# A weight piece's rounding term on GpSimd, five first loads on ScalarE's queue, and the input flag at step 88

## The chip, the cores and the metric

The kernel runs on one core of a Trainium2 chip. A core has five engines that run their own instruction queues in order: TensorE (PE in the profile; PEld is its weight load), VectorE (DVE), ScalarE (ACT), GpSimd (POOL) and SyncE (SP), which here only issues DMA transfers. The metric is the device time of one execution in microseconds (us); lower is better. Before the change it is 751.67 us, the median of 3 runs (749.25 to 754.2).

## The reference

Attention with a local window and a few global columns is followed by a feed-forward part with a gelu. There are 4 batches of 768 positions, 8 heads of 64, d_model 512 and d_ff 2048; the weights w_in and w_out are float64.

```python
scores = scale * np.matmul(q, k.transpose(0, 1, 3, 2))
is_global = pos[None, :] < int(n_global)
is_local = (rel >= 0) & (rel < int(n_local))
bias = -slopes[:, None, None] * dist[None, :, :]
scores = np.where(is_global | is_local, scores + bias, -1e9)
a = np.exp(scores - np.max(scores, axis=-1, keepdims=True))
a = a / (np.sum(a, axis=-1, keepdims=True) + 1e-09)
x = np.matmul(a, v)                      # heads side by side: 3072 x 512
h = x @ w_in
g = 0.5 * h * (1.0 + erf(h * inv_sqrt2))
return (g @ w_out).astype(np.float32)
```

## The kernel before

**Chunks and steps.** The 3072 positions are cut into 12 chunks of 256 (c), and the hidden 2048 columns into 8 slices of 256 (s). A step is one chunk with one slice: 96 steps, numbered T. In each step PE makes h = x·w_in for the slice (`m1`, L461, 24 matmuls), ScalarE makes the gelu gr (L471), GpSimd the rounded part gh (`hi_pool`, L145), VectorE the rest gl = gr − gh (L151), and PE adds both into the chunk's two accumulators (`m2`, L491, 24 matmuls). m1 runs one step ahead of m2. After a chunk's last slice ScalarE copies an accumulator to a tile o (L497) and issues its output transfer (L498). The tiles with the tag "o" share two buffers.

**Splitting.** Every product is made of three matmuls of a rounded part (hi) and a rest (lo) of each operand. Chunks 0 and 1 (`NATIVE`) do the attention in plain float32 instead. Attention for a chunk is scores (L332 in the first two chunks), row maximum on VectorE (L341), exponentials on ScalarE (L356), transposes on PE (L382), the copy pt to SBUF on ScalarE (L385 in the first two chunks), the product with v (av, L410), and for the later chunks a scaling by GpSimd (L369).

**The opening.** Steps 0 to 3 take the slices 0 and 1 of chunks 0 and 1, and the next twelve alternate between these chunks, so that each weight slice is used by both. Meanwhile the weights arrive: 32 pieces (8 slices of 4 pieces, w0_0 to w7_3, 512 KB each) of 64-bit words, loaded by SP (L156) into four buffers for the slices 0 to 6. `split_weights` turns a piece into float32: L180 takes the low words, reads them as unsigned numbers and scales them to the rounding term; L182 and L184 cut and shift the bits of the high words into a tile wb on VectorE; L186 adds the rounding term, so it waits for L180; ScalarE copies the result into its hi form (L192); VectorE subtracts (L151). SP's next load of a piece waits until L186 and L184 have read the buffer's last content.

**The limits and the flag.** n_local and n_global are loaded to all partitions (L55) and made into a penalty for the scores. The fast path holds only for certain inputs, so VectorE collects the largest row maximum (nmax) and a check over the weights' words (wand; the words are loaded a second time, c<-w, and checked at the even steps up to 80). `flag` reduces both to one number: a chain on VectorE (wmin, mx, ok, bad), a transpose on PE (flag_ps, L596), and three more steps on VectorE to flag_i. All engines then load flag_i (L750) and branch on it (L751) past a general path that isn't taken here.

**What sets the order.** The tile framework's scheduler orders each engine's instructions by its own model of time; within that, waits between engines are semaphores. Its decisions change with the code, so instructions that the source doesn't touch may move too.

The DECODE table gives the step in which the pieces of a slice are split (−6, −4, … 8), and START the step at which each chunk's attention begins.

Of the kernel before, what the change touches and what calls it, by code (L numbers as in the profile page):

```python
# [10 lines left out]
I32 = mybir.dt.int32  # L11
U32 = mybir.dt.uint32
AF = mybir.ActivationFunctionType
ALU = mybir.AluOpType
PSUM = bass.MemoryType.PSUM

B, H, S, D = 4, 8, 768, 64
P = 128
# [5 lines left out]
CT = 256  # L24
# [24 lines left out]
def dap(t, off, dims):  # L49
    return bass.AP(tensor=t.tensor, offset=t.offset + off, ap=[list(d) for d in dims])  # L50


def load_scalars(nc, pool, src, name):
    w = pool.tile([P, 2, 2], I32, name=name + "_w")
    nc.sync.dma_start(w.rearrange("p i t -> p (i t)"), src.bitcast(I32).partition_broadcast(P))  # L55
    f = pool.tile([P, 2, 2], F32, name=name + "_f")
    nc.vector.tensor_copy(f, w)
    r = pool.tile([P, 2], F32, name=name)
    lo, hi = f[:, :, 0], f[:, :, 1]
    nc.vector.scalar_tensor_tensor(out=r, in0=lo, scalar=0.0, in1=hi, op0=ALU.is_lt, op1=ALU.add)  # L60
    nc.vector.scalar_tensor_tensor(out=r, in0=r, scalar=4294967296.0, in1=lo, op0=ALU.mult, op1=ALU.add)
    return r[:, 0:1], r[:, 1:2]
# [6 lines left out]
class Fast:  # L69
# [30 lines left out]
    def consts(self):  # L100
        nc, const = self.nc, self.const
        self.nl, self.ng = load_scalars(nc, const, self.limits, "nn")
        self.ident = const.tile([P, P], F32, name="ident")
        make_identity(nc, self.ident)
# [62 lines left out]
    def split_weights(self, s):  # L167
        nc = self.nc
        if s == LATE:
            self.early.close()  # L170
            self.wts = self.ctx.enter_context(self.tc.tile_pool(name="wlate", bufs=1, side="right"))
        if s == NST - 1:
            self.words.close()
            self.wts = self.ctx.enter_context(self.tc.tile_pool(name="wlast", bufs=1))
        for nm, dst, shape in (("win", self.win, [P, 4, 256]), ("wout", self.wout, [P, 2, 512])):
            dst[s] = tuple(self.wts.tile(shape, F32R, name=f"{nm}{k}{s}") for k in "hl")
        for i in range(4):
            w = self.raw.pop((s, i, "w"))
            lw, hw = w[:, :, 0], w[:, :, 1]
            nc.scalar.activation(out=lw, in_=lw.bitcast(U32), func=AF.Copy, scale=2.0 ** -29)  # L180
            a = self.sm.tile([P, 512], I32, name=f"wb{s}_{i}", tag="o")
            nc.vector.tensor_scalar(out=a, in0=hw, scalar1=0x07FFFFFF, scalar2=3,  # L182
                                    op0=ALU.bitwise_and, op1=ALU.logical_shift_left)
            nc.vector.scalar_tensor_tensor(out=a, in0=hw, scalar=-0x40000000, in1=a,  # L184
                                           op0=ALU.bitwise_and, op1=ALU.bitwise_or)
            nc.vector.tensor_tensor(out=a, in0=a, in1=lw, op=ALU.add)  # L186
            af = a.bitcast(F32)
            if i < 2:
                hi, lo = (x[:, 2 * i:2 * i + 2, :].rearrange("p d f -> p (d f)") for x in self.win[s])
            else:  # L190
                hi, lo = (x[:, i - 2, :] for x in self.wout[s])
            nc.scalar.copy(hi, af)  # L192
            self.lo_dve(lo, af, hi)
# [21 lines left out]
    def load_qk(self, c, p):  # L215
        nc = self.nc
        b, cc = divmod(c, CPB)
        k0 = (b * H + 2 * p) * D * S
        first = cc == 0
        nb = 1 if first else 2  # L220
        if c in NATIVE:
            kr = self.es.tile([P, nb, 256], F32, name=f"kr{c}_{p}", tag="kn", bufs=4)
            qr = self.es.tile([P, CT], F32, name=f"qr{c}_{p}", tag="qn", bufs=4)
            if first:
                nc.sync.dma_start(kr[:, 0, :], dap(self.kT, k0, [[S, P], [1, 256]]))
            else:
                nc.sync.dma_start(kr[:, :, NG:256], dap(self.kT, k0 + cc * CT - 96, [[S, P], [P, 2], [1, 224]]))
                nc.sync.dma_start(kr[:, :, 0:NG], dap(self.kT, k0, [[S, P], [0, 2], [1, NG]]))
            nc.sync.dma_start(qr, dap(self.qT, k0 + cc * CT, [[S, P], [1, CT]]))
            self.raw[c, p] = (kr, qr, nb)  # L230
            return
        if p == 0 and (cc == 1 or c == len(NATIVE)):
            self.load_glob(b)
        kr = self.stg.tile([P, 2, nb, 256], F32, name=f"kr{c}_{p}", tag="stage", padded_shape=[P, 2, 2, 256])
        qr = self.stg.tile([P, 2, CT], F32, name=f"qr{c}_{p}", tag="qraw", bufs=1)
        for u in (0, 1):
            ps = slice(u * 64, u * 64 + 64)
            if first:
                nc.sync.dma_start(kr[ps, :, 0, :], dap(self.kT, k0, [[S, D], [D * S, 2], [1, 256]]))
            else:  # L240
                for j in range(2):
                    nc.sync.dma_start(
                        kr[ps, :, j, NG:256],
                        dap(self.kT, k0 + cc * CT + j * P - 96, [[S, D], [D * S, 2], [1, 224]]))
            nc.sync.dma_start(qr[ps], dap(self.qT, k0 + cc * CT, [[S, D], [D * S, 2], [1, CT]]))
        self.raw[c, p] = (kr, qr, nb)
# [285 lines left out]
                    if r == rr:  # L532
                        self.exps(c, bt)

    def run(self):
        self.load_qk(0, 0)
        self.consts()
        last = NCH * NST
        for c in NATIVE:
            for p in range(NP):  # L540
                if (c, p) != (0, 0):
                    self.load_qk(c, p)
                self.load_v(c, p)
            if c == 0:
                for s in range(3):
                    self.load_weights(s)
        for s in range(3, NST - 1):
            self.load_weights(s)
        for self.T in range(START[0] - 1, last):
            T = self.T  # L550
            for s in range(NST):
                if T == DECODE[s]:
                    if s == NST - 1:
                        self.load_weights(s)
                    self.split_weights(s)
            if 16 <= T < 80 and T % 2 == 0:
                self.check_load((T - 16) // 2)
            if 18 <= T < 82 and T % 2 == 0:
                self.check_words((T - 18) // 2)
            if 0 <= T + 1 < last:  # L560
                self.m1(T + 1, 0)
            self.att(T, "pt", 0)
            if 0 <= T + 1 < last:
                self.m1(T + 1, 1)
                self.gelu(T + 1)
            self.att(T, "s", 0)
            self.att(T, "pt", 1)
            if T >= 0:
                self.m2(T, 0)
            self.att(T, "av", 0)  # L570
            self.att(T, "s", 1)
            self.att(T, "exp", 0)
            self.att(T, "split", 0)
            if T >= 0:
                self.m2(T, 1)
            self.att(T, "av", 1)
# [65 lines left out]
def general(tc, qT, kT, v, w, out, limits):  # L642
# [3 lines left out]
    with ExitStack() as ctx:  # L646
        pool = lambda name, bufs=1, **k: ctx.enter_context(tc.tile_pool(name=name, bufs=bufs, **k))
        cst, bat, wk = pool("g_cst"), pool("g_bat"), pool("g_wk", 2)
        ps, pa, po = pool("g_ps", 4, space=PSUM), pool("g_pa", 2, space=PSUM), pool("g_po", 1, space=PSUM)
        nl, ng = load_scalars(nc, cst, limits, "g_nn")  # L650
        ident = cst.tile([P, P], F32, name="g_ident")
        make_identity(nc, ident)
# [88 lines left out]
def body(tc, qT, kT, v, w, limits, out):  # L741
    nc = tc.nc
    w = w.bitcast(I32)
    with tc.tile_pool(name="flagp", bufs=1) as fp:
        flag_i = fp.tile([1, 1], I32, name="flag_i")
        with ExitStack() as ctx:
            fast = Fast(tc, ctx, qT, kT, v, w, out, limits)
            fast.run()
            fast.flag(flag_i)
        fv = nc.values_load(flag_i, min_val=0, max_val=1)  # L750
        with tc.If(fv):  # L751
            general(tc, qT, kT, v, w, out, limits)
# [25 lines left out]
```

## Time and profile before

| | us |
|---|---|
| median of 3 runs | 751.67 (749.25 to 754.2) |
| the profiled execution | 753.28 |
| its span in the trace | 750.9 |
| PE busy in the span | 718.8 (96%) |
| DVE busy | 502.2 (67%) |
| ACT busy | 355.6 (47%) |
| POOL busy | 304.0 (40%) |

A row of the timeline gives start and length in us, then the engine, the line, the operation and its tiles (out<-in), and in brackets how long the engine had been idle before it and what ended that. A row of the waits gives who waited for whom, the us in total, how many times, and the longest. A row of the groups ends with busy us, the mean length of one in ns, and the idle us before them with what ended them. SPq and ACTq are the queues that issue transfers. The profile's shares are averages over the whole span; the opening, up to about 150 us, and the last 10 us look different from the rest.

### The profile page before, as it was taken

The numbers are of one execution on the slowest core, as the hardware profiler recorded it, in microseconds if no ns is written. First come the engines' busy times: TensorE is split into PE (matmuls) and PEld (weight loads), VectorE is DVE, ScalarE is ACT, GpSimd is POOL, SyncE is SP. The second block draws the span as 40 slices with busy tenths as digits, with TensorE's granted clock in tenths as the row PEclk, the third lists the DMA queues.
The fourth block names the chain that finished last, engine by engine and source line by source line (L and its number), as shares of the span: only waits on it lengthen the run. The fifth ranks groups of instructions, "written<-read, shape, count | busy, mean of one in ns | idle before, by whom it ended". The sixth has DMA issues, their size and how long they took to land.

```text
span 750.9 us, 13415 instructions
## 1 busy us (share of the span) xinstructions
PE 718.8 (96%) x4617; PEld 649.8 (87%) x4617; DVE 502.2 (67%) x1317; ACT 355.6 (47%) x906; POOL 304.0 (40%) x572
## 2 busy tenths in 40 slices
PE   5997989898999999999999999999999999999995
PEld 3776989787999999999889999999889999989984
DVE  6888887756857867856757867856658867633111
ACT  5646545455355355355355355355355455351110
POOL 2220033654544654543544554542533654431010
PEclk9999999999999999999999999999999999999998
DMA  8995523324434434334424434334334431100000
GB/s 245 269 242 176 173 81 113 98 64 120 119 101 137 115 101 127 97 88 132 119 82 136 119 101 122 100 92 124 99 103 117 127 110 43 44 15 1 29 1 32
DMA packets 74395, 80.91 MB, mean 108 GB/s; under 512 B 12368, under 2 KB 63056, under 8 KB 74320
## 3 DMA queue, kind: packets, MB, share of 16 engines
q1 hardware_dynamic: 70864, 73.69, 34.9%
q10 hardware_dynamic: 3456, 6.29, 2.3%
q8 instruction: 38, 0.62, 0.3%
q14 instruction: 37, 0.30, 0.1%
HBM read 73.66 MB, written 6.29 MB: 106 GB/s over the span
## 4 chain that ended last, share of the span: by engine, by line
PE 69%; DMA 10%; DVE 6%; ACT 6%; POOL 4%; issue 2%; SPq 1%; DVEq 0%; POOLq 0%; ACTq 0%
PE acc L491 29%; PE h L461 27%; DMA w<-w 7%; PE av L424 4%; PE s L336 4%; PE t L382 4%; POOL n L369 3%; ACT n L356 3%; DMA c<-w 2%; DMA kr<-kT 1%; POOL gh L145 1%; DVE wb L186 1%; ACT L356 1%; DVE wb L184 1%; ACT gr L471 1%
## 5 line engine op out<-in xcount | busy, mean ns | idle before, releaser
L461 PE MATMUL h<-xh,winh 128*128 128x256 f32 x768 | 219.7, 286 | 0.0
L461 PE MATMUL h<-xl,winh 128*128 128x256 f32 x768 | 218.6, 285 | 0.0
L461 PE MATMUL h<-xh,winl 128*128 128x256 f32 x768 | 217.3, 283 | 0.0
L491 PE MATMUL acc<-wouth,gh 128*128 128x512 f32 x384 | 155.0, 404 | 7.4 <-POOL gh L145 7.4
L491 PE MATMUL acc<-woutl,gh 128*128 128x512 f32 x384 | 152.4, 397 | 0.0
L461 PEld LDWEIGHTS h<-xh,winh 128*128 128x128 f32 x768 | 146.9, 191 | 2.4
L461 PEld LDWEIGHTS h<-xl,winh 128*128 128x128 f32 x768 | 146.9, 191 | 2.1
L461 PEld LDWEIGHTS h<-xh,winl 128*128 128x128 f32 x768 | 146.9, 191 | 0.2
L491 PE MATMUL acc<-wouth,gl 128*128 128x512 f32 x384 | 144.1, 398 | 1.2 <-DVE gl L151 1.2
L151 DVE TENSOR_TENSOR gl<-gr,gh 128x512 fp32r<-128x512 f32 x96 | 68.6, 715 | 92.5 <-POOL gh L145 92.5
L471 ACT ACTIVATE gr<-h 128x512 f32<-128x512 f32 x96 | 57.4, 598 | 149.8 <-PE h L461 109.9
L369 POOL TENSOR_SCALAR n<-n,su 128x256 f32<-128x256 f32 (+1 forms) x160 | 77.5, 504 | 87.7 <-DVE su L361 76.4
L145 POOL TENSOR_SCALAR gh<-gr 128x512 fp32r<-128x512 f32 x96 | 65.4, 681 | 108.9 <-ACT gr L471 108.9
L145 POOL TENSOR_SCALAR vt<-vr 128x256 fp32r<-128x256 f32 (+1 forms) x80 | 34.7, 435 | 154.1 <-DMA vr<-v 79.5
L356 ACT ACTIVATE n<-n,mn 128x256 f32<-128x256 f32 (+1 forms) x192 | 91.8, 480 | 7.8 <-DVE mn L341 7.5
L491 PEld LDWEIGHTS acc<-wouth,gh 128*128 128x128 f32 x384 | 73.2, 191 | 20.3 <-POOL gh L145 9.2
L491 PEld LDWEIGHTS acc<-wouth,gl 128*128 128x128 f32 x384 | 73.0, 190 | 18.2 <-DVE gl L151 2.9
L491 PEld LDWEIGHTS acc<-woutl,gh 128*128 128x128 f32 x384 | 73.2, 191 | 12.5
L431 ACT COPY t<-av 64x256 f32<-64x256 f32 x80 | 29.3, 366 | 99.3 <-PE av L424 98.8
L389 ACT CAST pt<-t 128x512 fp32r<-128x512 f32 (+1 forms) x80 | 44.4, 555 | 65.0 <-PE t L382 59.4
L341 DVE CUSTOM_DVE_ANT_0 n<-s,pen 128x256 f32<-128x256 f32 (+1 forms) x192 | 68.4, 391 | 5.1 <-PE s L336 3.5
L382 PE MATMUL t<-ident,n 128*128 128x128 f32 x352 | 61.2, 295 | 1.3 <-ACT gr L471 0.7
(87 smaller groups left out, 1060.9 us busy)
## 6 DMA issues: line engine op xcount, KB each, us to landing
w<-w SPq DMA_DIRECT2D x32, 512.0 KB, 4.6
c<-w SPq DMA_DIRECT2D x32, 512.0 KB, 3.7
kr<-kT SPq DMA_DIRECT2D x112, 112.0 KB, 2.7
qr<-qT SPq DMA_DIRECT2D x88, 128.0 KB, 3.1
vr<-v SPq DMA_DIRECT2D x48, 128.0 KB, 2.3
out<-o ACTq DMA_DIRECT2D x24, 256.0 KB, 2.2
kr<-kT SPq DMA_DIRECT2D x28, 128.0 KB, 2.8
vr<-v SPq DMA_DIRECT2D x32, 96.0 KB, 2.2
```

Source lines behind the costliest of these rows:

```text
L145: self.nc.gpsimd.tensor_scalar(out=out, in0=in_, scalar1=scale, scalar2=0.0, op0=ALU.mult, op1=ALU.add)
L151: self.nc.vector.tensor_tensor(out=out, in0=in_, in1=hi.bitcast(F32), op=ALU.subtract)
L336: nc.tensor.matmul(sp[:, j, :w], lhsT=qq[:, hh, j * P:(j + 1) * P], rhs=kt[:, t, 0 if first else j, :w], start=t == 0, stop=t == 1)
L341: nc.vector.tensor_tensor_reduce(out=nn[:, j, :w], in0=sp[:, j, :w], in1=pen, scale=-slope(h), scalar=3e38, op0=ALU.add, op1=ALU.min, accu ...
L356: ins = nc.scalar.activation(out=nn[:, j, :w], in_=nn[:, j, :w], func=AF.Exp, bias=mn[:, i:i + 1], scale=-1.0, accum_out=su[:, i:i + 1])
L369: nc.gpsimd.tensor_scalar(out=nn[:, j, :w], in0=nn[:, j, :w], scalar1=su[:, i:i + 1], scalar2=0.0, op0=ALU.mult, op1=ALU.add)
L382: nc.tensor.transpose(tp[:, i, :], nn[:, j, a * P:(a + 1) * P], self.ident)
L389: nc.scalar.copy(pt[:, :, 0, :], tp[:, :n, :])
L424: nc.tensor.matmul(av[:, j], lhsT=vt[:, vi], rhs=pt[:, i], start=start, stop=stop)
L461: nc.tensor.matmul(hp[:, f, :], lhsT=w[:, d, f * P:(f + 1) * P], rhs=x[:, d, :], start=n == 0, stop=n == 3 * NP - 1)
L471: self.table(nc.scalar.activation(out=gr, in_=hp, func=AF.Gelu))
L491: nc.tensor.matmul(acc, lhsT=g[:, f, ks], rhs=w[:, f, :], start=s == 0 and n == 0, stop=s == NST - 1 and n == 5)
```

## The change

Three edits. L180 becomes a GpSimd tensor_scalar of the same words (times 2^-29, plus 0). The transfer of the limits and the four q loads of chunk 0 are issued by ScalarE's queue instead of SP's. `flag` is called in step 88, ahead of that step's other work, instead of after the last step; the load of flag_i and the branch stay at the end.

```diff
 def load_scalars(nc, pool, src, name):
-    nc.sync.dma_start(w.rearrange("p i t -> p (i t)"), src.bitcast(I32).partition_broadcast(P))
+    nc.scalar.dma_start(w.rearrange("p i t -> p (i t)"), src.bitcast(I32).partition_broadcast(P))
...
             lw, hw = w[:, :, 0], w[:, :, 1]
-            nc.scalar.activation(out=lw, in_=lw.bitcast(U32), func=AF.Copy, scale=2.0 ** -29)
+            nc.gpsimd.tensor_scalar(out=lw, in0=lw.bitcast(U32), scalar1=2.0 ** -29, scalar2=0.0, op0=ALU.mult, op1=ALU.add)
...
-            nc.sync.dma_start(qr, dap(self.qT, k0 + cc * CT, [[S, P], [1, CT]]))
+            (nc.scalar if c == 0 else nc.sync).dma_start(qr, dap(self.qT, k0 + cc * CT, [[S, P], [1, CT]]))
...
-    def run(self):
+    def run(self, flag_i):
...
                     self.split_weights(s)
+            if T == 88:
+                self.flag(flag_i)
...
-            fast.run()
-            fast.flag(flag_i)
+            fast.run(flag_i)
```

Since the code before it grows by two lines, later lines count one or two higher after the change. The orders of the five engines differ from the start to about step 9 and from step 88 on; between them they are the same.

On ScalarE the opening begins so, with + for what is new and − for what is gone (qr0_0 to qr0_3 are the q tiles of chunk 0, w0_0 and w0_1 the first weight pieces, t and pt a head's transposed probabilities):

```order
+L229 DMA qr0_0_102<-qT 128x256
+L55 DMA nn_w_105<-limits 128x4
+L229 DMA qr0_1_151<-qT 128x256
+L229 DMA qr0_2_157<-qT 128x256
+L229 DMA qr0_3_163<-qT 128x256
 L356 ACT_TABLE_LOAD
 L356 ACTIVATE n0_0_264,su0_0_262<-n0_0_264,mn0_0_261 128x128
@@ -9,118 +14,88 @@
 L356 ACTIVATE n0_3_292,su0_1_284<-n0_3_292,mn0_1_283 128x128
 L356 ACTIVATE n0_3_292,su0_1_284<-n0_3_292,mn0_1_283 128x256
-L180 ACTIVATE w0_0_168<-w0_0_168 128x512
 L385 COPY pt0_0_310<-t0_0_306 128x384
```

The five issues stand ahead of the table load, and the first pt no longer has a weight piece ahead of it.

At steps 2 and 3, ScalarE's order before (w5_3 and w6_0 to w6_2 are pieces, winh and wouth the hi copies, gr2 and gr3 the gelus of these steps):

```order
L180 ACTIVATE w5_3_250<-w5_3_250 128x512
L180 ACTIVATE w6_0_252<-w6_0_252 128x512
L192 CAST winh5_1075<-wb5_1_1087 128x512
L192 CAST wouth5_1077<-wb5_2_1094 128x512
L471 ACTIVATE gr2_910<-h2_883 128x512
L180 ACTIVATE w6_1_254<-w6_1_254 128x512
L180 ACTIVATE w6_2_256<-w6_2_256 128x512
L471 ACTIVATE gr3_985<-h3_958 128x512
```

and GpSimd's order at the same place now:

```order
L145 TENSOR_SCALAR gh1_858<-gr1_860 128x512
L180 TENSOR_SCALAR w5_1_246<-w5_1_246 128x512
L180 TENSOR_SCALAR w5_2_248<-w5_2_248 128x512
L180 TENSOR_SCALAR w5_3_250<-w5_3_250 128x512
L145 TENSOR_SCALAR gh2_908<-gr2_910 128x512
L180 TENSOR_SCALAR w6_0_252<-w6_0_252 128x512
L180 TENSOR_SCALAR w6_1_254<-w6_1_254 128x512
L145 TENSOR_SCALAR gh3_983<-gr3_985 128x512
```

The pieces that stood ahead of gr2 and gr3 on ScalarE now stand ahead of gh2 and gh3 on GpSimd, with w6_0 behind gh2 instead of ahead of gr2.

At step 88, VectorE's order now (gl88 and gl89 belong to those steps; the rows between them are the flag's):

```order
L151 TENSOR_TENSOR gl88_8660<-gr88_8661,gh88_8659 128x512
L592 CAST wmin_8691<-wand_131 128x256
L593 TENSOR_REDUCE mx_8687<-wmin_8691 128x1
L594 TENSOR_SCALAR ok_8683<-mx_8687 128x1
L596 TENSOR_REDUCE bad_8695<-ok_8683 128x1
L600 TENSOR_REDUCE red_8699<-flag_ps_8697 1x1
L601 TENSOR_SCALAR red_8699<-red_8699 1x1
L602 CAST flag_i_58<-red_8699 1x1
L151 TENSOR_TENSOR gl89_8729<-gr89_8730,gh89_8728 128x512
```

They stood behind gl95 before. On PE, flag_ps now stands behind the 24 matmuls of step 88's m2, which themselves now follow step 87's directly, and ahead of step 89's m1. The tile wmin has the tag "o", and takes the buffer of chunk 10's first output.

## The prediction

> **What bounds the kernel now.** I read the windows first (start:end and length in us; busy time and instruction count of PE, PEld, DVE, ACT, POOL; clock; DMA share; GB/s), then the waits, then the timeline where PE stands still.
>
> ```profile
> span 750.9 us, 13415 instructions
> 0.00:10.00 10.00, 4.73 (x21) 2.98 (x21) 5.65 (x32) 3.27 (x10) 4.12 (x20) 1.00 0.62 187
> 10.00:20.00 10.00, 7.73 (x26) 5.09 (x25) 7.99 (x28) 8.14 (x25) 0.81 (x2) 1.00 1.00 312
> 20.00:30.00 10.00, 10.00 (x40) 8.06 (x38) 9.70 (x34) 5.75 (x17) 2.41 (x3) 1.00 1.05 257
> 50.00:60.00 10.00, 8.00 (x28) 5.59 (x27) 7.36 (x20) 5.93 (x15) 1.42 (x2) 1.00 0.96 262
> 60.00:70.00 10.00, 7.16 (x28) 5.81 (x27) 8.44 (x26) 6.89 (x19) 0.36 (x1) 1.00 0.47 147
> 70.00:80.00 10.00, 9.63 (x63) 9.63 (x64) 9.85 (x22) 6.28 (x12) 0.00 (x0) 1.00 0.52 172
> 200.00:600.00 400.00, 397.24 (x2681) 365.35 (x2679) 286.69 (x761) 196.92 (x521) 195.68 (x373) 1.00 0.39 111
> ...
> PE av L410 <- ACT pt L385: 7.5, 4, 3.2
> ACT w L180 <- DMA w<-w: 20.7, 13, 2.7
> ...
> PE acc L491 <- POOL gh L145: 4.0, 2, 2.1
> ```
>
> From 200 to 600 us PE works 397.24 of 400 us: nothing that this change touches can be won there. PE's idle time lies in the opening (5.27 + 2.27 + 2.00 + 2.84 us in four of these windows) and in the tail. Two waits own most of it: the first 75 us hold 7.5 us of PE waiting for pt copies of ScalarE (4 times), and 75 to 140 us hold 4.0 us of waiting for gh (twice). ScalarE's own queue explains the first: in those 75 us it stood 20.7 us at L180 until a weight piece had landed, with pt queued behind it.
>
> **The change, part by part.** The sum is made against the profiled execution, 753.28 us, of which 750.9 are the span; it lies 1.61 above the median of 751.67.
>
> *Start: five issues leave SP's queue, L180 leaves ScalarE's.*
>
> ```profile
> 0.75 0.41 SPq L225 DMA_DIRECT2D kr<-kT  x1
> 3.14 0.43 SPq L229 DMA_DIRECT2D qr<-qT  x1
> 7.01 2.10 SPq L156 DMA_DIRECT2D w<-w  x4
> ...
> 6.93 1.66 PE L332 MATMUL s<-kr,qr 64*128 64x128 f32 x8 [1.30 <-POOL qr L145]
> 13.00 0.68 ACT L180 ACTIVATE w<-w 128x512 int32<-128x512 uint32 x1 [1.23 <-DMA w<-w]
> 14.09 1.54 PE L410 MATMUL av<-vr,pt 128*128 128x64 f32 x6 [2.27 <-ACT pt L385]
> ```
>
> SP issues 13 transfers from 0.75 to 7.01, 0.48 each. Without five of them the first weight issue stands at 0.75 + 8 × 0.48 = 4.6 instead of 7.01. ScalarE is busy 3.27 of those first 10 us, so the five issues are covered there. The second qr, third in ScalarE's queue, goes out near 1.7 instead of 3.14, so the 1.30 us of PE waiting at 6.93 goes. The pt copy stood behind L180, which stood for a DMA until 13.00; without that it could start about 1.2 us earlier, and part of PE's 2.27 goes too. Bounds: −1.3 (first wait alone) and −3.6 (both whole); I take **−2.0**, since DVE is the next late engine (7.99 of the second window, 9.70 of the third). The Trainium skill, "DMA: Bandwidth & Descriptors", section "Issuing engines are not separate DMA queues", says that a second issuing engine saves only the issuing time; by it this term holds at most the 2.4 us of SP's issues, and the DMA share of 0.62 in the first window leaves room for them.
>
> *50 to 72 us: ScalarE no longer stands at L180.*
>
> ```profile
> 67.93 0.67 ACT L180 ACTIVATE w<-w 128x512 int32<-128x512 uint32 x1 [1.95 <-DMA w<-w]
> 70.37 1.54 PE L410 MATMUL av<-vr,pt 128*128 128x64 f32 x6 [3.21 <-ACT pt L385]
> ...
> L180 ACT ACTIVATE w<-w x18: 667/676/716, 13.0 to 71.7; 128x512 int32<-128x512 uint32 x18
> ...
> L186 DVE CUSTOM_DVE_ANT_0 wb<-w,wb 128x1024 uint16<-128x1024 uint16 x32 | 22.6, 713 | 0.4
> L184 DVE SCALAR_TENSOR_TENSOR wb<-w,wb 128x512 int32<-128x512 int32 x32 | 22.5, 709 | 0.2
> L182 DVE TENSOR_SCALAR wb<-w 128x512 int32<-128x512 int32 x32 | 14.0, 441 | 5.8 <-DMA w<-w 5.6
> L145 POOL TENSOR_SCALAR gh<-gr 128x512 fp32r<-128x512 f32 x10 | 8.2, 820 | 44.3 <-ACT gr L471 44.3
> ```
>
> PE's idle time here is 2.00 + 2.84 us in the two windows and 0.37 after, 5.2 in all. It would all go if ScalarE alone were late. But the step now runs on POOL beside DVE. No row shows it there; the nearest is POOL's tensor_scalar of the same 512 elements, gh, 0.82 on average and 0.62 where nothing stands in its way:
>
> ```profile
> L145 POOL TENSOR_SCALAR gh<-gr x10: 618/623/1406, 81.5 to 138.5; 128x512 fp32r<-128x512 f32 x10
> ...
> 96.17 1.17 POOL L145 TENSOR_SCALAR gh<-gr 128x512 fp32r<-128x512 f32 x1 [10.62 <-ACT gr L471]
> 96.18 0.69 DVE L151 TENSOR_TENSOR woutl<-wb,wouth 128x512 fp32r<-128x512 f32 x1
> 96.78 1.10 DVE L184 SCALAR_TENSOR_TENSOR wb<-w,wb 128x512 int32<-128x512 int32 x1
> ```
>
> Here gh and DVE's operations of two tensors take turns: gh ends 1.17 us after its start, and L184 takes 1.10 instead of its mean of 0.71. So I price L180 on POOL between 0.62 and 1.41, and take 0.82. Either way POOL carries 32 × 0.82 = 26 us where it was nearly idle. L186 needs it only after L182 and L184, 0.44 + 0.71 = 1.15 us after the piece has landed, so 0.82 is hidden there and 1.41 isn't. DVE pays 0.4 whenever it starts such an operation while POOL runs; L184, L186 and L151's subtraction (0.69) are 2.1 of the 2.5 us that a piece costs DVE, so I count one meeting for every second piece: of the 18 pieces up to 72 us, 9 × 0.4 = 3.6 us on an engine that has little room (9.85 of 10 from 70 to 80). Of the 5.2 us that leaves 1.6; what is late next is DVE itself, or a landing that DVE or POOL now waits for. I take **−1.5**, with bounds 0 and −5.2.
>
> The Trainium skill, "SBUF — State Buffer", section "Who interferes with whom", says the same more strictly: DVE and GpSimd share one pair of ports under an exclusive lock, and a DVE operation with two SBUF inputs keeps GpSimd from reading meanwhile. It speaks against this change, since ScalarE stands outside that lock; the trace's 1.17 and 1.10 agree. Were each of the 18 pieces hit, that would be 7.2 instead of 3.6, and the term nothing.
>
> *95 us: gr of the third step.*
>
> ```profile
> 95.50 0.59 ACT L471 ACTIVATE gr<-h 128x512 f32<-128x512 f32 x1
> 97.39 0.50 PE L491 MATMUL acc<-wouth,gh 128*128 128x512 f32 x1 [1.95 <-POOL gh L145]
> ```
>
> The chain is gr, gh, PE. Before, gr2_910 stands behind w5_3_250 and w6_0_252 on ScalarE; now its gh stands behind w5_3_250 alone on POOL. Its queue is shorter by a piece and two copies, so of 1.95 I take **−1.7**; bounds 0 (gh waits for the landing instead of gr) and −1.95.
>
> *134 us: the other wait for gh.*
>
> ```profile
> 129.86 5.83 POOL L369 TENSOR_SCALAR n<-n,su 128x256 f32<-128x256 f32 x8 [5.28 <-ACT w L180]
> 136.76 0.50 PE L491 MATMUL acc<-wouth,gh 128*128 128x512 f32 x1 [2.06 <-POOL gh L145]
> 137.72 0.63 PE L491 MATMUL acc<-woutl,gh 128*128 128x512 f32 x1
> ```
>
> Here gh is late because eight L369 run ahead of it on POOL, and POOL gets two L180 more in front of them. I take **−0.5**, with bounds +1.6 (two L180 on the path) and −2.06. After this wait PE's accumulations last 0.63 instead of the 0.50 and less before it, for some 3 us; that goes only if the wait goes whole.
>
> *Flag at step 88.*
>
> ```profile
> 696.50 2.75 PE acc L491 x12
> ...
> 698.54 0.34 ACTq L498 DMA_DIRECT2D out<-o  x1
> ...
> DMA to landing us min/median/max: 2.0/2.2/3.4
> ...
> 742.21 0.34 ACTq L498 DMA_DIRECT2D out<-o  x1
> 743.35 0.29 DVE L590 CAST wmin<-wand 128x256 f32<-128x256 int32 x1 [5.43 <-DMA out<-o]
> 744.63 0.27 PE L596 MATMUL flag_ps<-ident,bad 128*1 128x128 f32 x1 [3.22 <-DVE bad L594]
> ...
> L750 ACTq TENSOR_LOAD <-flag_i x1: 472/472/472, 745.6 to 745.6; - x1
> ```
>
> At the end the branch waits for the flag: from the last issue's end, 742.55, to the load at 745.6. With the flag long made, ScalarE loads at 742.55; the rest, 750.9 − 745.6 = 5.3 us of branch and end, stays. **−3.0**; bounds −2.0 (a load that some other queue begins later) and −3.1. What it costs at step 88: wmin takes the buffer of chunk 10's first output, whose transfer is issued at 698.54 and lands 2.2 us later, at 700.7 (the row of its landings stands under its issue). Then wmin to flag_ps takes 1.28 (743.35 to 744.63), so flag_ps can run at 702.0. PE's twelve accumulations take 2.75 from 696.50 by the chain of waits, and twelve more now stand in front of flag_ps: 702.0 too, with the next h queued behind. The two meet, so I take its own 0.27 and a little waiting, **+0.4**; bounds 0 and +1.6 (a landing of 3.4). DVE's next gl waits behind the same chain, but needs h first.
>
> Sum: −2.0 − 1.5 − 1.7 − 0.5 − 3.0 + 0.4 = −8.3, so 745.0 against 753.28; less the 1.61 by which that execution lies above the median, **743.4**.
>
> **The rivals.** *The opening gives nothing net.* The 20.7 us and more of waiting for landed weights move with the step into POOL's queue, where qr, the chunk's k and q, and gh stand behind it, and DVE's stretches eat the rest. For it: DVE is at 9.70 and 9.85 in two windows, and the same landings are waited for. Against: POOL has under 2.5 of 10 us of work in each quoted window from 10 to 80. The opening then gives 0 to −2: 753.28 − 2.6 − (0 to 2) − 1.6 = 747.1 to 749.1.
>
> *Slower: POOL and DVE collide at each piece.* L180 lasts 1.41, so L186 waits 0.26 beyond L184's end, and DVE pays 0.39 for a meeting: 0.65 for each of the 25 pieces up to w6_0_252 is 16 us, or 26 where L180 spans two such operations. DVE's idle time in the five quoted windows from 10 to 80 is 50 − 43.3 = 6.7. With that absorbed, PE's steady work starts 10 to 19 us later: 753.28 + (10 to 19) − 2.6 − 1.6 = 759 to 768. It decides once L180 exceeds 1.15 us. Against: gh, its nearest row, is at 0.82.
>
> *All ScalarE gaps go, and the slow accumulations with them.* −3.6 − 5.2 − 1.95 − 2.06 and −1.5 for the slow accumulations (eight of them, against the 2.75 for twelve at 696.50): 753.28 − 14.3 − 2.6 − 1.6 = 735.
>
> *The flag is no gain*: the load at the end is bound by something else, e.g. the last output's landing at 742.21 + 2.2 = 744.4. Then −3.0 shrinks to −1.2 or less: 745.2 to 746.4.
>
> **How the numbers follow.** Forecast 0.54 (738 to 748); nothing net 0.26; slower 0.08; all gaps 0.08; flag no gain 0.04. The likeliest gives 743.4. The range, 737 to 751, leaves out the slower rival and half of the all-gaps one, 0.12, and takes in the terms' bounds as far as they don't all fall together. One per cent, about what can be told from no change here, is 744.2 below and 759.2 above. Faster: three fifths of the forecast's case (its centre lies 0.8 below the bound), 0.33, and 0.08, 0.41 in all. Slower: 0.07 of the rival. Same: the rest, 0.52.
>
> **What would show it.** First weight issue near 4.6 instead of 7.01. L180's row on POOL with a median between 0.62 and 1.15, and L184's and L186's means near 0.85 to 0.9; past 1.0 the slower rival is at work. PE's wait for pt under 4 us in 75 instead of 7.5, and ScalarE's for weights gone. One wait for gh instead of two before 140. At 702 a PE wait for the flag under 1.6 us. ScalarE's flag load some 8 us before the earlier 745.6, directly behind its last issue. The forecast is wrong if a row "POOL w L180 waits for DMA" is followed by PE waits for gh or qr that weren't there, or if the time from the last issue to the end isn't near 5.6.

## The result, and the profile after

The changed kernel takes 746.7 us, the median of 20 runs, against 751.96 us of 20 runs of the kernel before: a ratio of 0.9929 (95% interval 0.9913 to 0.9946), 5.3 us or 0.7% faster. One of the 20 executions took 1372 us; it is left out of the ratio, and no run here explains it. The forecast was 743.4 us with a range of 737 to 751. The profiled execution took 746.23 us, of which 744.3 are the span.

The windows of the changed kernel (columns as in the prediction):

```profile
span 744.3 us, 13435 instructions
0.00:10.00 10.00, 4.30 (x19) 2.64 (x20) 5.84 (x33) 2.75 (x8) 4.25 (x20) 1.00 0.70 196
10.00:20.00 10.00, 9.66 (x35) 6.85 (x34) 9.03 (x28) 6.39 (x24) 5.39 (x6) 1.00 1.06 324
20.00:30.00 10.00, 10.00 (x37) 7.94 (x36) 10.00 (x31) 6.69 (x23) 3.68 (x6) 1.00 1.10 257
...
60.00:70.00 10.00, 8.07 (x33) 6.83 (x33) 9.97 (x27) 5.56 (x15) 2.17 (x4) 1.00 0.52 160
...
130.00:140.00 10.00, 8.01 (x40) 7.00 (x41) 6.70 (x14) 3.80 (x9) 9.43 (x13) 0.83 0.18 64
200.00:600.00 400.00, 397.94 (x2700) 366.46 (x2699) 289.54 (x766) 196.91 (x520) 198.15 (x372) 1.00 0.39 112
```

PE gained in the window from 10 to 20 us (9.66 instead of 7.73), VectorE is fuller (10.00 from 20 to 30 and 9.97 from 60 to 70, instead of 9.70 and 8.44), and from 130 to 140 PE still stands still for 2 us while POOL is full (9.43). Its waits of the first 75 us, then those of 75 to 140 us, and then the groups of a weight piece:

```profile
POOL w L180 <- DMA w<-w: 19.5, 10, 3.3
PE s L332 <- POOL qr L145: 5.6, 2, 4.0
PE av L410 <- ACT pt L385: 2.6, 3, 1.9
...
POOL w L180 <- DMA w<-w: 22.3, 9, 5.6
...
PE t L382 <- POOL n L369: 1.9, 2, 1.5
PE acc L491 <- POOL gh L145: 0.8, 2, 0.6
...
L180 POOL TENSOR_SCALAR w<-w 128x512 int32<-128x512 uint32 x32 | 27.4, 858 | 56.9 <-DMA w<-w 38.5 <-DVE wb L182 7.5 <-DVE wb L184 4.2
L184 DVE SCALAR_TENSOR_TENSOR wb<-w,wb 128x512 int32<-128x512 int32 x32 | 26.1, 816 | 0.4
L186 DVE CUSTOM_DVE_ANT_0 wb<-w,wb 128x1024 uint16<-128x1024 uint16 x32 | 24.7, 770 | 1.1 <-POOL w L180 0.6
L182 DVE TENSOR_SCALAR wb<-w 128x512 int32<-128x512 int32 x32 | 15.9, 497 | 2.3 <-DMA w<-w 2.3
```

The wait for landed pieces moved from ScalarE (20.7 us in the first 75) to POOL (19.5, and 22.3 more by 140), and PE's wait for pt fell from 7.5 to 2.6. L180 takes 0.86 on POOL; L184, L186 and L182 grew from 0.71, 0.71 and 0.44 to 0.82, 0.77 and 0.50.

Where the 6.6 us between the two spans lie is read from the first accumulation of a step. First the rows of step 7 and step 9 before (that of step 8 stands in the prediction) with the window behind step 8's start; then the rows of steps 7, 8 and 9 after with two windows, and the last issue with what follows it:

```profile
127.56 0.40 PE L491 MATMUL acc<-wouth,gh 128*128 128x512 f32 x1
142.15 0.40 PE L491 MATMUL acc<-wouth,gh 128*128 128x512 f32 x1
...
137.00:141.00 4.00, 4.00 (x12) 3.05 (x12) 4.00 (x10) 1.94 (x5) 0.86 (x2) 0.57 0.18 55
```

```profile
123.83 0.50 PE L491 MATMUL acc<-wouth,gh 128*128 128x512 f32 x1
136.75 0.50 PE L491 MATMUL acc<-wouth,gh 128*128 128x512 f32 x1 [0.65 <-POOL gh L145]
140.58 0.40 PE L491 MATMUL acc<-wouth,gh 128*128 128x512 f32 x1
...
132.00:136.00 4.00, 4.00 (x22) 3.85 (x20) 2.47 (x4) 1.10 (x2) 4.00 (x6) 0.57 0.21 65
137.00:141.00 4.00, 4.00 (x22) 3.44 (x22) 3.44 (x9) 2.59 (x8) 3.20 (x5) 1.00 0.17 41
...
739.29 0.34 ACTq L498 DMA_DIRECT2D out<-o  x1
L751 ACTq TENSOR_LOAD <-flag_i x1: 476/476/476, 739.7 to 739.7; - x1
L752 PEldq COMPARE_BRANCH  x1: 3317/3317/3317, 735.7 to 735.7; - x1
```

At step 7 the changed kernel is 3.7 us ahead (123.83 against 127.56); at step 8 nothing of it is left (136.75 against 136.76). That is not the last word: at step 9 the changed kernel is 1.6 us ahead again (140.58 against 142.15), at step 10 0.8 and at step 62 0.1. TensorE's granted clock averages 0.57 from 137 to 141 before, on step 8's accumulations (0.63 each); in the changed kernel it does so from 132 to 136, ahead of a wait for gh, and the accumulations behind it take 0.40.

From the last issue's end to the span's end it takes 744.3 − 739.63 = 4.7 us instead of 750.9 − 742.55 = 8.35: 3.7 us gained. The remaining 2.9 come in at steps 62 to 64, where the execution of before that was profiled took 17.2 us, and the other ten traces of this study 14.3 to 15.4 for the same two steps. So that part is a chance of one execution; its PE worked 8.27 of 10 us at a granted clock of 0.83 in the stretch from 525 to 535, the changed kernel's 9.56 at 1.00:

```profile
525.00:535.00 10.00, 8.27 (x45) 7.08 (x44) 4.05 (x13) 3.57 (x8) 5.11 (x12) 0.83 0.22 61
```

```profile
525.00:535.00 10.00, 9.56 (x70) 8.75 (x69) 6.41 (x19) 4.55 (x9) 5.79 (x14) 1.00 0.38 113
```

### The profile page after: what moved, and what is told of

It is laid out like the page before. It is cut to its first block, busy times and chain, and to the rows that moved or that the text cites. A ratio compares the mean times of both kernels' runs of the same rounds, so it can differ in the third digit from the quotient of the medians.

```text
span 744.3 us, 13435 instructions
## 1 busy us (share of the span) xinstructions
PE 719.6 (97%) x4617; PEld 648.9 (87%) x4617; DVE 514.6 (69%) x1317; ACT 338.0 (45%) x874; POOL 335.2 (45%) x604
## 4 chain that ended last, share of the span: by engine, by line
PE 71%; DVE 10%; DMA 6%; ACT 5%; POOL 5%; issue 2%; ACTq 0%; SPq 0%; POOLq 0%; DVEq 0%
PE acc L491 29%; PE h L461 29%; PE av L424 4%; PE s L336 4%; PE t L382 4%; POOL n L369 3%; ACT n L356 3%; DMA w<-w 2%; DMA kr<-kT 2%; DVE wb L186 2%; DMA c<-w 2%; DVE wb L184 2%; PE av L410 1%; DVE wb L182 1%; DVE n L341 1%
## 5 line engine op out<-in xcount | busy, mean ns | idle before, releaser
L491 PE MATMUL acc<-wouth,gh 128*128 128x512 f32 x384 | 153.8, 401 | 3.6 <-POOL gh L145 3.3
L491 PE MATMUL acc<-woutl,gh 128*128 128x512 f32 x384 | 151.2, 394 | 0.0
L491 PE MATMUL acc<-wouth,gl 128*128 128x512 f32 x384 | 142.9, 395 | 2.1 <-DVE gl L151 2.1
L369 POOL TENSOR_SCALAR n<-n,su 128x256 f32<-128x256 f32 (+1 forms) x160 | 77.2, 503 | 79.0 <-DVE su L361 67.0
L491 PEld LDWEIGHTS acc<-wouth,gl 128*128 128x128 f32 x384 | 72.1, 188 | 19.5 <-DVE gl L151 4.4
L491 PEld LDWEIGHTS acc<-wouth,gh 128*128 128x128 f32 x384 | 72.4, 189 | 16.6 <-POOL gh L145 5.5
L491 PEld LDWEIGHTS acc<-woutl,gh 128*128 128x128 f32 x384 | 72.5, 189 | 12.4
```

Source lines behind the costliest of these rows:

```text
L369: nc.gpsimd.tensor_scalar(out=nn[:, j, :w], in0=nn[:, j, :w], scalar1=su[:, i:i + 1], scalar2=0.0, op0=ALU.mult, op1=ALU.add)
L491: nc.tensor.matmul(acc, lhsT=g[:, f, ks], rhs=w[:, f, :], start=s == 0 and n == 0, stop=s == NST - 1 and n == 5)
```

## The experiments

**The flag alone.** The kernel before, with `flag` called at step 88.

```diff
+            if T == 88:
+                self.flag(flag_i)
...
-            fast.flag(flag_i)
```

> The kernel before with the flag moved to step 88 and nothing else. If the tail is what the change gives (the branch no longer waits for the flag: 9.88 us from the last accumulation to the end before, 6.2 after, with 0.1 to 0.3 lost at step 88), this alone is 3.3 to 3.6 us faster, a ratio near 0.9954. If the opening holds a lasting part of the measured 5.3 us, this falls short of it by 1.7 to 2 us; if it is all of the gain, the ratio is near 0.993.

Measured: 749.8 us, ratio 0.9968 (0.9953 to 0.9983), 2.4 us faster. Its tail is as short as the changed kernel's: 4.4 us from the last issue's end (741.86) to the end of its span (746.3). Its opening runs in the order of before and came out 1.2 us later by step 9, so 1 us between two profiles is not to be read as an effect. The interval is 1.3 to 3.5 us: it just reaches what the tail shows in the traces, and leaves 1.8 us or more of the 5.3 to the opening, the subject of the next run.

**The opening alone.** L180 on GpSimd and five issues on ScalarE, `flag` after the last step as before. The orders of all engines are those of the changed kernel up to step 87. Against the changed kernel:

```diff
-            if T == 88:
-                self.flag(flag_i)
...
+            fast.flag(flag_i)
```

> The other two edits without the flag: L180 on GpSimd and the five issues on ScalarE's queue. Theory (the lead is given back at step 8): the accumulation of step 7 starts 3 to 4 us earlier than before, that of step 8 within 0.3 us of before, and the time is within 1 us of before (ratio 0.9985 to 1.0). Rival (the opening's lead lasts): step 8 is also 2 us or more earlier, and the ratio is 0.9975 or below.

Measured: 749.9 us, ratio 0.9971 (0.9954 to 0.9987), 2.2 us faster. Step 7 starts its accumulation at 122.96, 4.6 us ahead of before; step 8 at 136.31, 0.45 ahead. So most of the lead is given back there, as the theory had it, but 1.1 us of it are there again at step 10, and the time is not within 1 us of before: some two fifths of the whole gain come with these two edits (the interval is 1.0 to 3.5 us). The two runs add up to 4.6 of the 5.3.

**Slice 7's rounding terms on ScalarE.**

```diff
-            nc.gpsimd.tensor_scalar(out=lw, in0=lw.bitcast(U32), scalar1=2.0 ** -29, ...)
+            if s == NST - 1:
+                nc.scalar.activation(out=lw, in_=lw.bitcast(U32), func=AF.Copy, scale=2.0 ** -29)
+            else:
+                nc.gpsimd.tensor_scalar(out=lw, in0=lw.bitcast(U32), scalar1=2.0 ** -29, ...)
```

> The changed kernel, but the rounding term of the four pieces of slice 7 stays on ScalarE (28 pieces on GpSimd, 4 on ScalarE), so that GpSimd's eight L369 of chunk 2 have no piece ahead of them. Theory: they stood behind pieces 1 and 2 of slice 7, which landed late, so L369 starts 2 to 3 us earlier than at 130.3 and step 8's accumulation at 134 to 135 instead of 136.75; of that 1.5 to 2.5 us stay to the end, a ratio to before of 0.990. Rival (step 8 is set by VectorE's decode and the landing of slice 7, wherever the rounding term is made): step 8 stays at 136 to 137 and the ratio at 0.993.

Measured: 744.52 us, ratio 0.9909 (0.9874 to 0.9945). POOL in the changed kernel, and then in this one (where three more lines of code make L361, L369 and L491 L364, L372 and L494), by the timeline:

```profile
126.06 0.81 POOL L180 TENSOR_SCALAR w<-w 128x512 int32<-128x512 uint32 x1 [2.29 <-DMA w<-w]
129.40 0.83 POOL L180 TENSOR_SCALAR w<-w 128x512 int32<-128x512 uint32 x1 [2.52 <-DMA w<-w]
130.32 5.79 POOL L369 TENSOR_SCALAR n<-n,su 128x256 f32<-128x256 f32 x8
136.08 0.61 POOL L145 TENSOR_SCALAR gh<-gr 128x512 fp32r<-128x512 f32 x1
```

```profile
122.15 0.40 PE L494 MATMUL acc<-wouth,gh 128*128 128x512 f32 x1
126.16 5.02 POOL L372 TENSOR_SCALAR n<-n,su 128x256 f32<-128x256 f32 x8 [5.25 <-DVE su L364]
131.16 1.04 POOL L145 TENSOR_SCALAR gh<-gr 128x512 fp32r<-128x512 f32 x1
132.25 0.50 PE L494 MATMUL acc<-wouth,gh 128*128 128x512 f32 x1 [1.30 <-POOL gh L145]
```

In the changed kernel the eight L369 stand behind two pieces of slice 7 that land at 126.06 and 129.40, and gh stands behind them. Without these two they start at 126.16, as soon as su is made, and step 8 begins at 132.25. VectorE's su also moved ahead: in the changed kernel it stood behind piece 1's L186, which needs POOL's L180. So at step 8 the rival (step 8 is set by VectorE's decode wherever the term is made) falls. The time doesn't decide: its interval holds the theory's 0.990 and the rival's 0.993, and the profiled execution was 1.5 us ahead of the changed kernel's at the first step's accumulation already (79.96 against 81.42), where the orders are still the same.

**L180 back on ScalarE**, with the queue and the flag edits kept.

```diff
-            nc.gpsimd.tensor_scalar(out=lw, in0=lw.bitcast(U32), scalar1=2.0 ** -29, ...)
+            nc.scalar.activation(out=lw, in_=lw.bitcast(U32), func=AF.Copy, scale=2.0 ** -29)
```

> The changed kernel with L180 back on ScalarE: what the move of L180 itself is worth. Theory: the opening's start keeps its lead of about 1.5 us, ScalarE waits for landings again (PE for pt 6 to 8 us in the first 75 us), and since the lead of the changed kernel is lost at step 8 anyway, the time is within 1 us of the changed kernel's (ratio to before 0.992 to 0.9955). Rival (GpSimd collides with VectorE at a lasting cost): faster than the changed kernel, 0.991 or below. Rival (the move gives 2 us or more that stay): 0.996 or above.

Measured: 753.57 us, ratio 1.0013 (0.999 to 1.0037): the gain of the flag is lost in the opening. The second rival's number (0.996 or above) comes out, but the move of L180 is not all that it measures: the scheduler made yet another order here, with pt behind two pieces that are waited for in turn. ScalarE's and PE's rows by the timeline:

```profile
46.61 0.68 ACT L180 ACTIVATE w<-w 128x512 int32<-128x512 uint32 x1 [2.86 <-DMA w<-w]
52.63 0.66 ACT L180 ACTIVATE w<-w 128x512 int32<-128x512 uint32 x1 [2.81 <-DMA w<-w]
54.17 0.57 ACT L385 COPY pt<-t 128x512 f32<-128x512 f32 x1
54.79 1.97 PE L410 MATMUL av<-vr,pt 128*128 128x64 f32 x8 [6.39 <-ACT pt L385]
```

PE's wait for pt is 11.4 us in the first 75 us, 6.39 of it here. So the run shows what a weight piece ahead of pt in ScalarE's queue can cost; it does not price the move alone.

**One queue.** The changed kernel with all five loads on SP again.

```diff
-    nc.scalar.dma_start(w.rearrange("p i t -> p (i t)"), ...)
+    nc.sync.dma_start(w.rearrange("p i t -> p (i t)"), ...)
...
-            (nc.scalar if c == 0 else nc.sync).dma_start(qr, ...)
+            nc.sync.dma_start(qr, ...)
```

> The changed kernel with the limits and the four q loads of chunk 0 issued by SP again. Theory: five issues on a second queue gain nothing, since with eight transfers under way SP waits before each further issue (7.08 instead of the forecast 4.6 for the first weight issue), so the first weight issue stands at 7.0 here too, the second scores at 6.9 instead of 7.29, and the time is within 1 us of the changed kernel's, ratio to before 0.992 to 0.994. Rival (the second queue has its part in the opening's lead): step 7's accumulation 1 us or more later than 123.8 and a ratio of 0.9945 or above.

Measured: 749.76 us, ratio 0.9962 (0.9943 to 0.998), 2.5 us slower than the changed kernel by the two ratios, whose intervals just overlap: the rival's numbers. The first weight issue is at 7.02, against 7.08 with two queues, so no transfer of a weight starts later; but dozens of rows of PE, ScalarE and VectorE stand in another order, which the scheduler chose. PE's wait for pt is 7.5 us in the first 75 us instead of 2.6, and step 7 starts at 127.51.

**Two issues.** Only the limits and the first q load go through ScalarE's queue; PE's and GpSimd's orders are the changed kernel's, and the others' but for these loads.

```diff
-            (nc.scalar if c == 0 else nc.sync).dma_start(qr, ...)
+            (nc.scalar if c == 0 and p == 0 else nc.sync).dma_start(qr, ...)
```

> The changed kernel with only the limits and the first q load on ScalarE's queue, the other three q loads on SP: 11 issues on SP instead of 8. Theory (SP's pace is set by landings once eight are under way): the first weight issue comes at 6.0 to 6.6, earlier than with five moved (7.08), although SP issues three more ahead of it, and the second q lands earlier than 6.4. Rival (issues cost 0.48 each on either queue together): 13 x 0.48 from 0.75, so 7.0 again. Rival (the forecast's sum, 0.48 for each of SP's own): 6.0. Time within 1 us of the changed kernel's.

Measured: 745.71 us, ratio 0.9913 (0.988 to 0.9946). First the waits of SP's queue in the changed kernel's first 8 us, with its issues; then this run's:

```profile
SPq L286 <- DMA vr<-v: 1.5, 1, 1.5
SPq L225 <- DMA qr<-qT: 0.7, 1, 0.7
SPq L286 <- DMA kr<-kT: 0.6, 1, 0.6
...
2.22 0.44 SPq L286 DMA_DIRECT2D vr<-v  x1
3.37 0.33 SPq L225 DMA_DIRECT2D kr<-kT  x1
5.17 0.37 SPq L286 DMA_DIRECT2D vr<-v  x1
7.08 1.89 SPq L156 DMA_DIRECT2D w<-w  x4
```

```profile
5.59 0.43 SPq L286 DMA_DIRECT2D vr<-v  x1
6.06 2.04 SPq L156 DMA_DIRECT2D w<-w  x4
```

With two issues moved, SP's 11 issues run without a pause, 0.48 each, and the first weight issue comes at 6.06. With five moved it waits 2.8 us for earlier landings, from its fifth issue on, when eight had been issued on the two queues together; 0.75 + 8 × 0.48 + 2.8 = 7.4 (7.08 in the trace) eats the whole saving. For eleven issues the forecast's way of counting, 0.48 each, gives 6.0 as well, so it is the 2.8 us in the changed kernel that speak against it. The piece that comes 1 us earlier is worth 0.2 us at step 7 (123.66 against 123.83) and no more later. So with the same order the start of these loads hardly matters; in the run with one queue, what is left to explain its loss is the order. That was not tried by itself: no kernel here has the changed kernel's order with one queue.

**The rounding twice.** A second pass of GpSimd over each term, in place (times 1, plus 0), as an extra cost.

```diff
             nc.gpsimd.tensor_scalar(out=lw, in0=lw.bitcast(U32), scalar1=2.0 ** -29, ...)
+            nc.gpsimd.tensor_scalar(out=lw, in0=lw, scalar1=1.0, scalar2=0.0, op0=ALU.mult, op1=ALU.add)
```

> The changed kernel with a second pass of GpSimd over each rounding term (times 1, plus 0, in place): the step takes about 1.65 us per piece instead of 0.83, which tests the rival that said it turns the change slower once it exceeds 1.15. That rival: L186 waits 0.5 for it at each piece and VectorE is hit twice, so step 7's accumulation comes 8 to 15 us later than 123.8 and the time is 754 or more. Theory: GpSimd idles 57 us ahead of L180 and L186 stands behind other work on VectorE, so only part of it shows: step 7's accumulation 2 to 6 us later, and since step 8 waits for GpSimd's L369 behind two such pairs, 1 to 4 us slower than the changed kernel (ratio to before 0.994 to 0.999).

Measured: 756.31 us, ratio 1.0057 (1.003 to 1.0084). The rival's numbers come out (step 7 at 134.57, 10.7 us later), but not by its mechanism: up to step 7 VectorE stands 0.5 us for the second pass, at L186. VectorE's load tells it. From 10 us to step 7's accumulation, windows of before, of the changed kernel and of this run:

```profile
10.00:127.50 117.50, 108.03 (x545) 91.56 (x544) 99.65 (x249) 68.55 (x169) 23.61 (x34) 1.00 0.67 191
```

```profile
10.00:124.00 114.00, 109.53 (x548) 92.34 (x547) 108.13 (x244) 53.54 (x148) 49.23 (x62) 1.00 0.67 186
```

```profile
10.00:134.50 124.50, 113.08 (x547) 95.37 (x548) 119.21 (x249) 53.58 (x148) 75.93 (x91) 0.97 0.62 172
...
100.00:106.00 6.00, 5.32 (x21) 4.94 (x22) 5.96 (x9) 1.84 (x3) 4.25 (x6) 0.50 0.39 112
```

VectorE is busy 99.65, 108.13 and 119.21 us: the change stretched its work by 8.5 us, the second pass by 11.1 more. It is idle 17.9 us in the first, 5.9 in the second and 5.3 in the third. The change used up most of VectorE's slack in the opening; behind that, 11.1 us more of VectorE's work go with 10.7 us at step 7. That the one makes the other is likely, but not shown alone: dozens of PE's and VectorE's rows stand in another order here, and from 100 to 106 us the granted clock was 0.50 with PE busy 5.32 of 6 us.

**Slice 7 on ScalarE, one queue.** The diffs of the third and the fifth run together:

```diff
+            if s == NST - 1:
+                nc.scalar.activation(out=lw, ...)
...
+            nc.sync.dma_start(qr, ...)
```

> The changed kernel with slice 7's rounding terms on ScalarE and all loads on SP: what is left of the change is the 28 pieces on GpSimd and the flag. Theory: as with slice 7 on ScalarE and both queues, step 8's accumulation at 132 to 133 and a ratio to before of 0.989 to 0.992. Rival (that gain came from a lucky order of the opening): step 8 at 135 or later and 0.993 or above.

Measured: 748.73 us, ratio 0.9943 (0.9924 to 0.9962). Step 8 is at 135.91, and 0.9943 is the rival's number: against the run with one queue it gains 1 us, while by the ratios the order of one queue costs 2.6 us again (the intervals overlap). Since its step 7 was late already (125.93), it is the distance from step 7 to step 8 that compares across orders:

| slice 7's rounding term | from step 7's first accumulation to step 8's, us |
|---|---|
| on GpSimd | 12.92 (changed), 13.35, 12.74, 13.12 |
| on ScalarE | 9.20 (before), 9.49, 10.10, 9.67, 9.98, 9.37 |

(In the order of this section, without the run with a second pass, which has 11.30; the last value is that of the next run.) Between kernels that differ in this alone, the pieces ahead of L369 cost 2.8 us (twice) and, with the next run, 3.7 at this step. In the times they are worth 1.4 to 2.7 us by the three pairs of ratios, each with intervals that overlap.

**Two issues, slice 7 on ScalarE.** Both edits in one kernel:

```diff
+            if s == NST - 1:
+                nc.scalar.activation(out=lw, ...)
...
+            (nc.scalar if c == 0 and p == 0 else nc.sync).dma_start(qr, ...)
```

> The changed kernel with two edits at once: only the limits and the first q load on ScalarE's queue, and slice 7's rounding terms on ScalarE. The instruction order is that of the run with slice 7 on ScalarE, but for those three loads. Theory (the two effects are apart: loads that come 1 us earlier are worth 0.2 us by step 7, slice 7 on ScalarE 2 to 3 us from step 8 on): first weight issue at 6.06, step 8's accumulation at 131.5 to 132.5, ratio to before 0.988 to 0.992, faster than both kernels. Rival (the gain of slice 7 on ScalarE, measured in 5 runs with an interval of 0.987 to 0.9945, was partly chance): 0.9925 or above.

Measured: 744.4 us, ratio 0.9877 (0.985 to 0.9903): faster than the kernel before by 8.5 us, and than the changed one (0.9929, 0.9913 to 0.9946) by an interval that doesn't touch. One of the forecast places came out, the first weight issue at 6.06. The other didn't: step 8 is at 135.03 in the profiled execution, which was already 2.6 us later at the first step's m1 than the run with slice 7 on ScalarE (72.84 against 70.20), with PE and GpSimd in the same order; its step from 7 to 8 is 9.37. So single executions of nearly one order lie up to 3.5 us apart at step 7 (122.15 and 125.66).

## Why the prediction was right, and where not

The time lies in the range and the sign is right, but the forecast gain was 8.3 us and the measured one 5.3. The range reaches to 751, nearly the time before, so that the time lies in it says little of the working. Up to step 8 the four terms of the opening promised 5.7 us, and nothing of them was left there. By its steps:

*The start, −2.0: right in size, wrong in cause.* At the seventh head's scores PE is 1.4 us ahead (16.55 against 17.97). The first weight issue did not come at 4.6 but at 7.08, and PE's wait for the second qr grew from 1.30 to 1.65. The step that failed is the count of issues at 0.48 each with nothing between them: it left out that SP waits for landings once the two queues together have issued eight. The Trainium skill's sentence that a second issuing engine saves issuing time ("DMA: Bandwidth & Descriptors", "Issuing engines are not separate DMA queues") gave the same 2.4 us; the runs show 1.0 with two issues moved and none with five. What moved was pt, no longer behind L180: PE's row that waited 2.27 waits 0.34.

```profile
7.29 1.66 PE L332 MATMUL s<-kr,qr 64*128 64x128 f32 x8 [1.65 <-POOL qr L145]
12.68 1.54 PE L410 MATMUL av<-vr,pt 128*128 128x64 f32 x6 [0.34 <-ACT pt L385]
```

*50 to 72 us, −1.5.* The wait for pt fell as forecast, but the lead at the first step's accumulation is 2.4 us (81.42 against 83.79), 1.0 more than at the start. The row of VectorE was right as the reason: I took 0.4 at every second piece, 0.2 a piece; the runs give 8.5 us over the 29 pieces up to step 7, 0.3 a piece. The lock of which the Trainium skill speaks ("SBUF — State Buffer", "Who interferes with whom") agrees with L180 at 0.65 to 1.22 and with VectorE's longer rows.

*95 us, −1.7: right.* The wait of 1.95 is gone, and the lead grows from 2.4 to 4.2 us there (step 2 at 93.23 against 97.39).

*134 us, −0.5: the step that failed.* The forecast said that POOL gets two L180 more ahead of L369, and priced them at their own 0.82 each, with +1.6 as the bound. What it left out is that POOL also waits for their landing, 2.29 and 2.52 us, and that VectorE's su had moved behind L186 of such a piece. The step cost +3.7 at step 8's first accumulation instead of giving 0.5; at step 10 the lead is 0.8 (150.12 against 150.89), so 3.0 of it are gone there. The run with slice 7 on ScalarE shows it: 12.9 us between the two steps become 10.1. The prediction also said that the slow accumulations behind the wait go only if the wait goes whole. They went although step 8 began no earlier, since the stretch at the lower clock lay ahead of them; that gave back 1.6 us by step 9.

*The flag, −3.0 + 0.4: right, 3.7 and 0.2 in the profiled executions; alone it measured 2.4 (1.3 to 3.5).* wmin waited for its buffer until 697.53, and PE's next h came at 698.83, as the last accumulation ended. A step's m2 has twelve matmuls, as the prediction counts, not the 24 of the kernel's description; the lead of 3.1 us at step 87 is 2.9 at step 95. The end is 0.7 us shorter than forecast, since PE's branch, 3.3 to 3.5 us in both traces, now runs while ScalarE still copies (735.7 instead of 746.2):

```profile
L751 PEldq COMPARE_BRANCH  x1: 3514/3514/3514, 746.2 to 746.2; - x1
```

*The rivals.* The first was that the opening gives nothing net, with the weight waits in POOL's queue ahead of qr, k, q and gh; it named 747.1 to 749.1, and the measured 746.7 lies nearer to that than to 743.4. At step 8 it is what happened, by L369 and gh; yet the opening alone was measured at 2.2 us, so of the 5.7 us that I put on it some 40% came. The slower rival had the right place (VectorE), but L180 took 0.86, under its 1.15; with a second pass the kernel is slower than before, though at 756.31 and not at its 759 to 768. The baseline explains 0.3 us of the 3.3 by which the forecast time was missed: the median before was 751.67 of three runs and is 751.96 of twenty. The 2.3 us that the execution of before lost at steps 62 to 64 are in no term of the sum.

*The prediction's own signs of being wrong* came in part. PE's waits for gh before 140 fell from 4.0 to 0.8 us, but PE now waits 1.9 us there for L369's n, behind two rows of L180 that waited for a landing; and the time from the last issue to the end was 4.7 instead of 5.6. What stays open is where the opening's 2.2 us lie: in the changed kernel's trace 0.7 us of lead are there at step 16 and 0.1 at step 62, in that of the opening alone 1.1 and 1.7.

## What to carry to other kernels

An instruction that waits for a transfer took its wait along to the queue that it was moved to (20.7 us on ScalarE, 19.5 on POOL): price the landing times of everything behind it there, not its own length. An engine that shares its access with a fuller one isn't free because it is idle; look at how much idle time the fuller one has left in that stage, here 17.9 us, and what each piece takes of it. And a check that feeds a branch at the end can be made earlier where its input is ready: that gain, 3.7 us in the trace and 2.4 measured alone, was the part that needed nothing else.

## What the runs showed of the hardware that was not expected

Five issues moved to a second queue moved the first weight issue by nothing (7.08 against 7.01), two moved it by 1.0 (6.06): in this kernel SP's issues waited 2.8 us for earlier landings from the ninth issue of the two queues on, and the q loads' landing grew from 2.9 to 4.6 us. And GpSimd's pass over a piece went with about 0.3 us more of VectorE's work in this mix (8.5 us over 29 pieces), though VectorE waited only 0.6 us in all for its result by 140 us. TensorE's granted clock averaged 0.57 over 4 us near step 8 before and after alike; where that stretch fell ahead of a wait for gh (0.57 from 132 to 136), PE still stood idle for 0.65 us behind it, and the accumulations took 0.40 instead of 0.63.
